# One core, linear attention and a gated SSM: conversion of the second weight unit moved ahead, two tensors turned in 64x64 quarters, a branch that places PE's program, and another order of PSUM banks

## The chip, the cores and the metric

One core of a Trainium2 chip runs the kernel. The metric is device microseconds of one execution, median of several. TensorE is PE here (its weight loads PEld), VectorE is DVE, ScalarE ACT, GpSimd POOL; SyncE (SP) issues most of the DMAs.

## The reference

```python
q, k, v, alpha: (4, 8, 768, 48)                 # batch, heads, steps, width
for t in range(768):
    state = alpha[:, :, t, :, None] * state + einsum('bhd,bhe->bhde', k[:, :, t], v[:, :, t])
    y[:, :, t] = einsum('bhd,bhde->bhe', q[:, :, t], state)
x = y.transpose(0, 2, 1, 3).reshape(4, 768, 384)
val, gate = split(x @ w_in)                     # w_in (384, 1024)
h = exp(A_log)[0] * h + val[:, t]               # along the steps
out = (silu(gate) * hs) @ w_out                 # w_out (512, 384)
```

The weights come as 64-bit floats and are converted on the chip.

## The kernel before, in words

The 768 steps of each batch are cut into three chunks of 256, so there are N = 12 chunks, m or n = 0 to 11. All matmuls are in fp32. For a chunk, the raw q, k and alpha come in with (head, block of steps) on the partitions and are turned so that the width stands there: by `turned` on PE against an identity for chunks 0 to 2 and the alphas of 3 (`alphas`, `straighten` and `turn_over` call it), by DVE's 32x32 transposes (`turn`, L613) later. `turned` has two ways: PE's transpose (L720 and L721), or two matmuls of 64 columns each per step (L725). ScalarE copies the result out (`copy_turned`, L732). Then, on DVE: `scan_P` (L648) makes the running product of the alphas, `scan_V` (L667) the running inverse, `scaled_k` (Zk, L632) and `scaled_q` (Zq, L623) the scaled tensors. `junk` is a check on ScalarE.

On PE: `scores(m)` multiplies Zk with Zq (L816) into two pairs of banks (s0, s1 and two of the common banks); `masks(m)` (L826 in chunks 0 to 2, L832 later) brings them to SBUF, on DVE under a mask and on ScalarE as they are; `values` (L849), `states` (L881) and `carried` (L862) sum the output of the attention in the banks y0 and y1 (for chunk 0 `first_values`, `first_states`, `first_carried` and `first_join`, which copies to xT); `third` is carried, values, carried and the copies and DMAs (L980) that lay the result out as xT. `project(n, cc)` (L1005), cc = 0 to 3, multiplies xT with one weight unit: a bank for the values, read by a scan on DVE (hh, L1014), and one for the gate, read by ScalarE (sg, L1025). `output(n)` and `output_parts(n)` (L1090) multiply with w_out; the second needs fewer matmuls and adds parts on DVE (L1117 to L1119), the last of them when the next chunk has begun (`next(outs)`).

A weight unit is converted by `low` (ScalarE, L556), `high` (DVE, L562 and L564) and `add_low` (POOL, L569); `load_w` (SP, L456) brings its bits. The load of unit 1 waits for a small memset on DVE (L1196).

No scheduler is at work: each engine runs its instructions in the order in which the code writes them, and `go(count)` takes the next steps of DVE's list of products. PSUM has eight banks: mm0 to mm3, y0, y1 (a and b below) and s0, s1 (s and t). Each call of `bank()` without a tag takes the next letter of a string written by hand, `taken`; who takes a bank waits until its last reader is done. `addr_align(256, x, max_nops=0)` puts PE's next instruction at place x of a block of 256, by a branch over the gap; before, it stands only at L1009, in seven projects (cc = 2).

Of the kernel before, what the change touches and what calls it, by code (L numbers as in the profile page):

```python
# [343 lines left out]
FLOOR = 1e-31  # L344
BLOCK_PLACE = 218


@with_exitstack
def fast(
# [221 lines left out]
    def convert(i):  # L571
        if i not in lows:
            low(i)
        high(i)
        add_low(i)
# [98 lines left out]
    def products(m):  # L674
# [19 lines left out]

    taken = iter("0321032103231023" "1023102310231023" "102310231023" "10"
# [16 lines left out]

    turned_by_transpose = ((0, "k"), (1, "a"), (1, "k"), (1, "q"), (3, "a"))

# [66 lines left out]

    def turn_over(m, name, to):
        for js in halves:
            copy_turned(to, js, turned(m, name, js, bank()))
# [9 lines left out]
    def keep_warm(n, w):  # L794
        t = bank("y0")
        for _ in range(n):
            nc.tensor.matmul(t[:, 0:w], nc.const_aps.tensor(0.0, [C, C], FP32),
                             nc.const_aps.tensor(0.0, [C, w], FP32), start=True, stop=True,
                             skip_group_check=True)
# [20 lines left out]
    def masks(m, cs=range(G)):  # L820
        sc = [[t[:, 0:4 * (L + D)].rearrange("p (h x) -> p h x", h=4) for t in pair] for pair in scs[m]]
        mb = mask[:, None, :]
        if m < NG:
            for c in cs:
                for i in range(2):
                    nc.vector.tensor_mul(As[i][:, c], sc[c][i][:, :, D:], mb.to_broadcast([C, 4, L]))  # L826
                for i in range(2):
                    nc.scalar.activation((K0, dS[m % 2][1])[i][:, c, :, 0:D], sc[c][i][:, :, 0:D], AF.Copy)
            return
# [341 lines left out]

    keep_warm(3, 256)
    first_alphas()
    for t in sums:
# [10 lines left out]
    for c in range(G):  # L1185
        scaled_k(0, tk, V, c)
        scaled_q(0, tq, P, c)
    tk, tq = plain("k"), plain("q")
# [6 lines left out]
    high(0)  # L1195
    nc.vector.memset(wbits[units[1]][0:1, 0, 0, 0:1, 0], 0)  # L1196
    load_w(units[1], nc.sync)
    add_low(0)
    copy_turned(tk, halves[1], part)
    first_values(True)  # L1200
    st = states(0)
    part = turned(1, "q", halves[0], bank())
    first_states(st)
    copy_turned(tq, halves[0], part)
    nc.scalar.activation(raws["a"][0:1, 0:1], sums[3][0:1, 0, 0:1], AF.Copy)
    load_steps("a", 2, [nc.sync])
# [8 lines left out]
    first_carried((2, 3))  # L1215
    part = turned(1, "q", halves[1], bank(), False)
    first_join()
    low(1)
    copy_turned(tq, halves[1], part)
    nc.scalar.activation(a_dec, a_log, AF.Exp)  # L1220
    nc.scalar.activation(spare, minus, AF.Silu)
    load_v(2, nc.sync)
    junk(0)

# [12 lines left out]
    for n in range(N):  # L1237
        m = n + 1
        if n == 0:
            V = scan_V(1, P)  # L1240
            high(1)
            fs_late = [project(n, 0)]
            add_low(1)
            alphas(2)
            scaled_k(1, tk, V)
            scaled_q(1, tq, P)
            low(2)
            fs_late.append(project(n, 1))
            convert(2)
            first(m)  # L1250
            tk = straighten(2, "k")
            P = scan_P(2)
            tq = straighten(2, "q")
# [62 lines left out]
        else:  # L1316
            ahead = n > 2
            if n == 2:
                go(1)
            else:  # L1320
                if m + 1 < N:
                    go(1)
                    load_raw("k", n + 3, nc.sync)
                go(2 if ahead else 1)
                next(outs, None)
            if n == N - 2:
# [138 lines left out]
```

## Time and profile before

| | |
|---|---|
| median of 3 runs | 272.77 us (272.77, 273.12, 270.95) |
| profiled execution | 272.92 us, span 270.9 us |
| busy: PE, PEld, DVE, ACT, POOL | 97%, 86%, 88%, 42%, 57% of the span |
| chain that ended last | PE 71%, DVE 17%, DMA 4%, issue 4% |
| moved by DMA | 41.23 MB, mean 152 GB/s |

How to read the lines: in a timeline a row has its start and length in us, engine, line, operation, out<-in and count; in brackets is the idle time of the engine before it and what ended it. A row of waits has the total, the count and the longest. PE records two instructions for each fp32 matmul, so 6 matmuls are x12. The row PEclk has the granted clock of PE in tenths, 9 being full.

### The profile page before, as it was taken

How to read it: one execution, taken by the hardware profiler on the slowest of the kernel's cores; microseconds unless marked ns; L12 is line 12 of the kernel's file. 1: busy time of each engine (PE TensorE's matmuls, PEld its weight loads, DVE VectorE, ACT ScalarE, POOL GpSimd, SP SyncE). 2: the span in 40 equal slices, each digit the busy share in tenths (PEclk: the TensorE clock that was granted, in tenths of full speed). 3: DMA queues.
4: the chain of work that ended last, by engine and by line, in shares of the span. 5: the costliest groups of instructions: out<-in, count | busy, mean ns of one | idle time of the engine just before them, and what ended most of it. 6: DMA issues, size and time to landing. Idle time of an engine off the chain costs nothing.

```text
span 270.9 us, 10035 instructions
## 1 busy us (share of the span) xinstructions
PE 263.5 (97%) x4172; PEld 232.9 (86%) x4172; DVE 239.1 (88%) x326; ACT 112.4 (42%) x272; POOL 154.4 (57%) x195
## 2 busy tenths in 40 slices
PE   8999999999999799999999999999999999999994
PEld 6988888876688688998988988988978989989884
DVE  7979998998999978999999999999999996793452
ACT  3667766462342341731631812713533714414121
POOL 8122323175259745795975895995594995736110
PEclk9999999999999799999999999999999999999999
DMA  6938984998980694189299298498595550211201
GB/s 174 322 123 260 293 174 154 229 204 175 255 202 4 161 222 109 31 211 224 74 230 219 60 235 200 91 224 183 124 229 140 114 162 2 61 43 29 76 6 59
DMA packets 52307, 41.23 MB, mean 152 GB/s; under 512 B 27392, under 2 KB 50944, under 8 KB 52256
## 3 DMA queue, kind: packets, MB, share of 16 engines
q1 hardware_dynamic: 49472, 37.53, 56.7%
q0 software_dynamic: 1536, 2.20, 3.1%
q10 hardware_dynamic: 1248, 0.79, 1.2%
q8 instruction: 36, 0.59, 0.9%
q14 instruction: 15, 0.12, 0.1%
HBM read 32.54 MB, written 4.72 MB: 138 GB/s over the span
## 4 chain that ended last, share of the span: by engine, by line
PE 71%; DVE 17%; DMA 4%; issue 4%; ACT 1%; SPq 1%; POOL 1%; DVEq 0%; POOLq 0%; ACTq 0%
PE mm L1005 25%; PE mm L1090 10%; PE s L1005 7%; PE y L1005 5%; DVE P L648 4%; DMA raw_q<-in_q_dram 4%; PE mm L1041 4%; PE y L1090 3%; PE s L816 3%; PE mm L816 2%; DVE k L613 2%; DVE al L613 2%; PE s L881 2%; PE y L849 2%; PE y L862 2%
## 5 line engine op out<-in xcount | busy, mean ns | idle before, releaser
L1005 PE MATMUL mm<-xT,w_in 128*128 128x256 f32 x384 | 88.9, 383 | 0.7 <-DVE o_sb L1118 0.6
L1005 PEld LDWEIGHTS mm<-xT,w_in 128*128 128x128 f32 x384 | 71.8, 190 | 11.8 <-DVE o_sb L1118 1.0
L1027 POOL TENSOR_TENSOR f_last<-sg,hh 128x256 f32<-128x256 f32 x36 | 28.9, 808 | 30.9 <-DVE hh L1014 18.7
L1025 ACT ACTIVATE sg<-mm 128x256 f32<-128x256 f32 x29 | 11.1, 384 | 56.2 <-PE mm L1005 53.9
L903 POOL TENSOR_TENSOR sum<-sum,dS 128x192 f32<-128x192 f32 x30 | 27.3, 909 | 5.7 <-ACT dS L890 3.8
L667 DVE TENSOR_TENSOR_SCAN V<-al,ends 128x1028 f32<-128x1028 f32 x12 | 28.3, 2358 | 0.4
L648 DVE TENSOR_TENSOR_SCAN P<-al,lower 128x1028 f32<-128x1028 f32 x12 | 28.3, 2355 | 0.3
L1005 PE MATMUL s<-xT,w_in 128*128 128x256 f32 x120 | 28.0, 379 | 0.0
L1005 PEld LDWEIGHTS s<-xT,w_in 128*128 128x128 f32 x120 | 22.7, 190 | 2.8
L980 POOL DMA_DIRECT2D xT<-yst x44 | 22.6, 519 | 3.5 <-ACT yst L977 3.2
L569 POOL TENSOR_TENSOR w_in<-w_in,wr 128x768 int32<-128x768 int32 x4 | 7.3, 1824 | 25.7 <-DVE wr L564 16.1
L1090 PE MATMUL mm<-w_out,f_last 128*128 128x192 f32 x80 | 17.9, 348 | 1.9 <-DVE wobits L832 1.8
L613 DVE STREAM_TRANSPOSE q<-raw_q 128x1024 f32<-128x1024 f32 x9 | 18.3, 2036 | 0.9 <-DMA raw_q<-in_q_dram 0.9
L613 DVE STREAM_TRANSPOSE k<-raw_k 128x1024 f32<-128x1024 f32 x9 | 18.4, 2043 | 0.0
L632 DVE TENSOR_TENSOR Zk<-k,V 128x1024 f32<-128x1024 f32 (+1 forms) x14 | 18.0, 1286 | 0.1
L1025 ACT ACTIVATE sg<-s 128x256 f32<-128x256 f32 x13 | 5.0, 384 | 31.3 <-PE s L1005 28.1
L1014 DVE TENSOR_TENSOR_SCAN hh<-a_dec,hh,mm 128x256 f32<-128x256 f32 x21 | 15.5, 736 | 1.6 <-PE mm L1005 1.6
L1005 PE MATMUL y<-xT,w_in 128*128 128x256 f32 x72 | 16.5, 379 | 0.0
L613 DVE STREAM_TRANSPOSE al<-raw_a 128x1024 f32<-128x1024 f32 x8 | 16.4, 2050 | 0.0
L623 DVE TENSOR_TENSOR Zq<-q,P 128x1024 f32<-128x1024 f32 (+1 forms) x14 | 16.0, 1142 | 0.3
L1090 PEld LDWEIGHTS mm<-w_out,f_last 128*128 128x128 f32 x80 | 13.7, 197 | 2.8 <-DVE wobits L832 2.0
L1005 PEld LDWEIGHTS y<-xT,w_in 128*128 128x128 f32 x72 | 13.7, 190 | 1.9
(232 smaller groups left out, 587.1 us busy)
## 6 DMA issues: line engine op xcount, KB each, us to landing
out_dram<-o_sb SPq DMA_DIRECT2D x23, 192.0 KB, 3.7
v<-in_v_dram SPq DMA_DIRECT2D x22, 192.0 KB, 4.2
raw_k<-in_k_dram SPq DMA_DIRECT2D x18, 184.0 KB, 6.1
raw_q<-in_q_dram SPq DMA_DIRECT2D x18, 184.0 KB, 4.9
raw_k<-in_k_dram SPq DMA_DIRECT2D x18, 176.0 KB, 6.4
raw_q<-in_q_dram SPq DMA_DIRECT2D x18, 176.0 KB, 5.0
wbits<-in_moe_w_in_dram SPq DMA_DIRECT2D x8, 384.0 KB, 5.1
raw_a<-in_alpha_dram SPq DMA_DIRECT2D x16, 184.0 KB, 5.5
```

The lines of the kernel that those rows point to most:

```text
L613: nc.vector.transpose(out=by_runs(to).rearrange("p h c j -> p h j c"), in_=raws[name][:, 0:4 * ROW].rearrange("p (h j d) -> p h j d", h=4, ...
L623: nc.vector.tensor_mul(Zqs[m % 2][:, ds(u0, n), :, D:].rearrange("p u h t -> p h u t"), t[:, :, at].rearrange("p h (u t) -> p h u t", t=L) ...
L632: nc.vector.tensor_mul(Zks[m][:, ds(c0, n)].rearrange("p c h t -> p h c t"), t[:, :, at].rearrange("p h (c t) -> p h c t", t=C), V[:, :, 1 ...
L648: nc.vector.tensor_tensor_scan(out=P, data0=al[:, 0:4 * GP], data1=lower.rearrange("p h t -> p (h t)"), initial=0.0, op0=ALU.mult, op1=ALU ...
L667: nc.vector.tensor_tensor_scan(out=V[:, ::-1], data0=al[:, 1:4 * GP + 1][:, ::-1], data1=ends.rearrange("p h t -> p (h t)")[:, ::-1], init ...
L903: nc.gpsimd.tensor_add(Ss[j][:, :, 0:D], Ss[j - 1][:, :, 0:D], part)
L980: engines[n % len(engines)].dma_start(out=xT[to, a], in_=st[rows, i, e])
L1005: nc.tensor.matmul((pv, pg)[vg], w_ins[cc][:, kk, vg, :], xT[:, kk, :], start=(kk == 0), stop=(kk == NK - 1))
L1014: nc.vector.tensor_tensor_scan(out=hh, data0=a_dec[:, cc:cc + 1].to_broadcast([C, GC]), data1=pv, initial=prev_h[cc][:, GC - 1:GC] if n % ...
L1025: nc.scalar.activation(sg, pg, AF.Silu)
L1027: f = lambda: engine.tensor_mul(fs[n][cc], sg, hh)
L1090: nc.tensor.matmul(o, a[:, k], b[k] if type(b) is list else b[:, k], start=start and k == 0, stop=k == KC - 1, skip_group_check=True)
```

## The change

- In the opening, the memset and the load of weight unit 1 move from behind `add_low(0)` to behind the first Zk; `high(1)`, `low(1)` and `add_low(1)` move ahead of `scan_P(1)`. Both halves of q of chunk 1 are turned together, and by transposes; `junk(0)` goes ahead of `first_join`. One `low(2)` less is written, since `convert(2)` has it, and `convert(2)` goes ahead of project(0, 1), `scan_P(2)` ahead of the scores of chunk 1.
- Alpha and k of chunk 2 are turned in quarters: 32 matmuls on 64x64 tiles in two banks, each bank copied out whole. q of chunk 2 is turned by transposes, in banks y0 and y1.
- `masks` has another order of its copies and multiplications in chunks 0 to 2.
- `taken` has another order of banks at the output of chunk 2 and the projects of chunks 3, 5 and 8.
- In chunk 3 the last output additions of chunk 2 go ahead of `scan_V(5)`.
- PE branches to place 31 of a block behind `keep_warm`.

```diff
+OPENING_PLACE = 31
...
-    taken = iter("0321032103231023" "1023102310231023" "102310231023" "10"
-                 "23012301" "23" "2301" "ab" "2s3t0123" "23" "01" "23ba"
-                 "st23ab23" "23" "23ab" "01" "2s3tab23" "23" "ab" "2310"
+    taken = iter("0321032103231023" "102310ab10231023" "102310231023" "10"
+                 "23012301" "23" "0132" "ab" "0st12301" "23" "01" "23ba"
+                 "st23ab23" "23" "23ab" "01" "2st3ab23" "23" "ab" "2310"
                  "st230123" "23" "01" "23ba" "st23ab23" "23" "23ab" "01"
-                 "2s3tab23" "23" "ab" "2310" "st230123" "23" "01" "23ba"
+                 "2st3ab23" "23" "ab" "2310" "st230123" "23" "01" "23ba"
...
-    turned_by_transpose = ((0, "k"), (1, "a"), (1, "k"), (1, "q"), (3, "a"))
+    turned_by_transpose = ((0, "k"), (1, "a"), (1, "k"), (1, "q"), (2, "q"), (3, "a"))
+    turned_by_quarters = ((2, "a"), (2, "k"))
...
     def turn_over(m, name, to):
+        if (m, name) in turned_by_quarters:
+            raw = steps_of(name, m)
+            parts = [t.rearrange("p (j x) -> p j x", x=64) for t in bank_pair()]
+            for j in range(NJ):
+                for i, r in ((0, 0), (1, 1), (1, 0), (0, 1)):
+                    rows = ds(64 * r, 64)
+                    nc.tensor.matmul(parts[r][ds(64 * i, 64), j], raw[rows, ds(i * ROW + j * D, 64)],
+                                     ident[rows, rows], start=True, stop=True, skip_group_check=True)
+            for r, part in enumerate(parts):
+                nc.scalar.activation(by_runs(to)[:, :, ds(16 * r, 16)],
+                                     part.rearrange("p j (c h) -> p h c j", h=4), AF.Copy)
+            return
...
                 for i in range(2):
+                    if m == 1:
+                        nc.scalar.activation((K0, dS[m % 2][1])[i][:, c, :, 0:D], sc[c][i][:, :, 0:D], AF.Copy)
                     nc.vector.tensor_mul(As[i][:, c], sc[c][i][:, :, D:], mb.to_broadcast([C, 4, L]))
-                for i in range(2):
-                    nc.scalar.activation((K0, dS[m % 2][1])[i][:, c, :, 0:D], sc[c][i][:, :, 0:D], AF.Copy)
+                    if m != 1:
+                        nc.scalar.activation((K0, dS[m % 2][1])[1 - i][:, c, :, 0:D], sc[c][1 - i][:, :, 0:D], AF.Copy)
...
     keep_warm(3, 256)
+    nc.tensor.addr_align(256, OPENING_PLACE, max_nops=0)
     first_alphas()
...
         scaled_k(0, tk, V, c)
+        if not c:
+            nc.vector.memset(wbits[units[1]][0:1, 0, 0, 0:1, 0], 0)
+            load_w(units[1], nc.sync)
         scaled_q(0, tq, P, c)
...
-    nc.vector.memset(wbits[units[1]][0:1, 0, 0, 0:1, 0], 0)
-    load_w(units[1], nc.sync)
     add_low(0)
...
-    part = turned(1, "q", halves[0], bank())
+    parts = [turned(1, "q", js, bank()) for js in halves]
+    high(1)
     first_states(st)
-    copy_turned(tq, halves[0], part)
-    nc.scalar.activation(raws["a"][0:1, 0:1], sums[3][0:1, 0, 0:1], AF.Copy)
+    low(1)
+    add_low(1)
+    for js, part in zip(halves, parts):
+        copy_turned(tq, js, part)
+        if js.start == 0:
+            nc.scalar.activation(raws["a"][0:1, 0:1], sums[3][0:1, 0, 0:1], AF.Copy)
...
-    part = turned(1, "q", halves[1], bank(), False)
+    junk(0)
     first_join()
-    low(1)
-    copy_turned(tq, halves[1], part)
...
-    junk(0)
...
             V = scan_V(1, P)
-            high(1)
             fs_late = [project(n, 0)]
-            add_low(1)
             alphas(2)
             scaled_k(1, tk, V)
             scaled_q(1, tq, P)
-            low(2)
+            convert(2)
             fs_late.append(project(n, 1))
-            convert(2)
+            P = scan_P(2)
             first(m)
             tk = straighten(2, "k")
-            P = scan_P(2)
...
-                go(2 if ahead else 1)
-                next(outs, None)
+                go(1)
+                if n == 3:
+                    next(outs)
+                go(1)
+                if n > 3:
+                    next(outs, None)
```

DVE's order in the opening, from the masks of chunk 0 to Zq of chunk 1 (Zq_118), before. w_in_96 and w_in_97 are units 0 and 1, wide_S and sum the states of chunk 0:

```order
L826 TENSOR_TENSOR AK<-mm,mask 128x4x64
L562 TENSOR_SCALAR w_in_96<-wbits_100 128x768
L564 TENSOR_SCALAR wr<-wbits_100 128x768
L1196 MEMSET wbits_101 1x1
L952 TENSOR_TENSOR wide_S_72<-s_327,wide_S_71 128x4x48
...
L667 SCALAR_TENSOR_TENSOR V<-al_130,ends 128x1028
L658 COPY lower<-P 128x4
L562 TENSOR_SCALAR w_in_97<-wbits_101 128x768
L564 TENSOR_SCALAR wr<-wbits_101 128x768
L1014 SCALAR_TENSOR_TENSOR hh<-a_dec,mm 128x256
L632 TENSOR_TENSOR Zk<-k,V 128x4x2x128
L623 TENSOR_TENSOR Zq_118<-q,P 128x4x4x64
```

The same stretch of DVE with the change:

```order
L842 TENSOR_TENSOR AK<-mm,mask 128x4x64
L563 TENSOR_SCALAR w_in_96<-wbits_100 128x768
L565 TENSOR_SCALAR wr<-wbits_100 128x768
L563 TENSOR_SCALAR w_in_97<-wbits_101 128x768
L565 TENSOR_SCALAR wr<-wbits_101 128x768
L968 TENSOR_TENSOR wide_S_72<-s_331,wide_S_71 128x4x48
...
L668 SCALAR_TENSOR_TENSOR V<-al_130,ends 128x1028
L659 COPY lower<-P 128x4
L1030 SCALAR_TENSOR_TENSOR hh<-a_dec,mm 128x256
L633 TENSOR_TENSOR Zk<-k,V 128x4x2x128
L624 TENSOR_TENSOR Zq_118<-q,P 128x4x4x64
```

The two conversions of unit 1 have moved ahead of the states of chunk 0, and the memset (L1205 there) further up, behind the first Zk.

PE's order from the end of chunk 0's carried (y) to the scores of chunk 1, before:

```order
L943 MATMUL y_388<-Zq_117,wide_S_73 64x64
L725 MATMUL mm<-ident,raw_q 64x128 x8
L1005 MATMUL mm<-xT,w_in_96 128x256 x6
L725 MATMUL mm<-ident,raw_a 64x128 x16
L1005 MATMUL mm<-xT,w_in_97 128x256 x6
L816 MATMUL s_620<-Zq_118,Zk 64x112
```

and with the change:

```order
L959 MATMUL y_390<-Zq_117,wide_S_73 64x64
L1021 MATMUL mm<-xT,w_in_96 128x256 x6
L791 MATMUL mm<-ident,raw_a 64x64 x32
L1021 MATMUL mm<-xT,w_in_97 128x256 x6
L830 MATMUL s_639<-Zq_118,Zk 64x112
```

The second half of q (8 matmuls) no longer stands between chunk 0 and its projection, and the 16 matmuls of alpha of chunk 2 have become 32 small ones.

## The prediction

> **What bounds the kernel now.** I read the page first: busy shares and the granted clock by slice.
>
> ```profile
> PE 263.5 (97%) x4172; PEld 232.9 (86%) x4172; DVE 239.1 (88%) x326; ACT 112.4 (42%) x272; POOL 154.4 (57%) x195
> PEclk9999999999999799999999999999999999999999
> ```
>
> TensorE (PE) is the bound, so only two things shorten the kernel: less PE work in a stage where PE waits for nobody, or a PE wait taken away. One slice, the fourteenth, has a clock below full. So next the waits of PE, longest first, and PE's timeline at the long ones.
>
> ```profile
> PE mm L1090 <- DVE wobits L832: 1.8, 1, 1.8
> ...
> 87.36 0.95 PE L816 MATMUL mm<-Zq,Zk 48*64 48x112 f32 x32
> 90.13 0.92 PE L1090 MATMUL mm<-w_out,f_last 128*128 128x192 f32 x4 [1.82 <-DVE wobits L832]
> ...
> 199.04 1.56 PE L1005 MATMUL mm<-xT,w_in 128*128 128x256 f32 x6 [0.61 <-DVE o_sb L1118]
> ```
>
> In 270.9 us PE waits long in two places: at 88.31, between the scores of chunk 4 and the output of chunk 2, and 0.61 us at the projection of chunk 8. The first has a tail. The windows (columns: length, then busy time and count of PE, PEld, DVE, ACT and POOL, then granted clock, DMA share, GB/s) show it:
>
> ```profile
> 88.00:90.00 2.00, 0.30 (x15) 0.09 (x4) 1.97 (x6) 1.22 (x4) 1.96 (x4) 1.00 0.18 48
> 90.00:92.00 2.00, 1.87 (x9) 1.88 (x10) 2.00 (x3) 0.33 (x1) 1.98 (x4) 0.77 0.51 125
> 92.00:94.00 2.00, 2.00 (x8) 2.00 (x7) 2.00 (x2) 0.66 (x2) 0.26 (x2) 0.50 1.16 271
> 94.00:96.00 2.00, 2.00 (x13) 2.00 (x12) 1.90 (x4) 0.97 (x3) 0.74 (x1) 0.87 1.09 229
> ```
>
> Right behind the idle time the clock is 0.77, 0.50 and 0.87 in three windows of 2 us: 2 x (0.23 + 0.50 + 0.13) = 1.72 us of PE time lost. The 0.61 us wait at 199.04 has no such tail on the clock row. Together the first wait costs 1.82 + 1.72 = 3.54 us.
>
> **The banks (term A).** The wait is for PSUM. The output of chunk 2 takes banks 2 and 3 first, and those hold the second pair of score blocks of chunk 4, which VectorE (DVE) reads last, at the end of this row:
>
> ```profile
> 85.54 0.38 ACT L1025 ACTIVATE sg<-mm 128x256 f32<-128x256 f32 x1 [2.27 <-PE mm L1005]
> ...
> 85.93 0.73 DVE L1014 TENSOR_TENSOR_SCAN hh<-a_dec,hh,mm 128x256 f32<-128x256 f32 x1
> ...
> 89.66 0.41 DVE L832 TENSOR_TENSOR wobits<-mm,mask 128x256 f32<-128x256 f32 x1
> ```
>
> 89.66 + 0.41 = 90.07; PE goes on at 90.13. After the change this output starts in banks 0 and 1, last read by the gate and the scan of project(2, 3), at 85.92 and 86.66, both before PE has finished the scores at 88.31. So the wait ends, and nothing else holds PE there. On PE alone that is 3.54 us.
>
> Can DVE follow? It is the next engine, and PE would run into it. DVE's own waits in the next blocks are its room:
>
> ```profile
> 99.50 0.69 DVE L1014 TENSOR_TENSOR_SCAN hh<-a_dec,mm 128x256 f32<-128x256 f32 x1 [1.29 <-PE mm L1005]
> ...
> 102.09 0.69 DVE L1014 TENSOR_TENSOR_SCAN hh<-a_dec,mm 128x256 f32<-128x256 f32 x1 [0.49 <-PE mm L1005]
> ...
> 110.69 0.42 DVE L832 TENSOR_TENSOR A<-mm,mask 128x256 f32<-128x256 f32 x1 [0.34 <-ACT K L831]
> ...
> 130.10 0.42 DVE L832 TENSOR_TENSOR wobits<-mm,mask 128x256 f32<-128x256 f32 x1 [0.16 <-ACT K L831]
> ...
> 130.96 0.92 PE L1090 MATMUL mm<-w_out,f_last 128*128 128x192 f32 x4
> ```
>
> These waits are for work that PE releases, and an earlier PE takes them away: 1.29 + 0.49 + 0.34 + 0.16 = 2.28 us by the masks of chunk 6. There the output of chunk 4 still starts in banks 2 and 3: PE may start once the DVE row ends (130.52) and did so at 130.96, 0.44 later. So by chunk 4 PE can keep 2.28 + 0.44 = 2.7 us of the 3.54. That is the value I take; the ends are 1.82 (the idle time alone) and 3.54. The three output additions on DVE that now stand before scan_V(5) cost nothing: DVE does them anyway, and PE needs their banks only at project(3, 1) and later.
>
> **Chunk 8 (term B).** Project(8, 1) first writes bank 3, which the o_sb addition frees; now it starts in t and takes bank 3 for its second half, three matmuls later, which is 1.56 us by that row. The 0.61 us go: I take 0.6, with 0 as the other end, if DVE is late by more than that. In projects 3 and 5 the same swap removes nothing, since PE does not wait there.
>
> **The opening (term C).** Here PE gets less work, but DVE decides. The turning by pairs of 64-column matmuls, and two rows for 64x64 tiles, in the chain of waits:
>
> ```profile
> 32.09 3.64 PE mm L725 x64
> ...
> 42.20 0.47 PE y L849 x32
> ```
>
> Two tensors in 3.64 us, 1.82 each. Quarters are 64 records of 64 columns on 64x64 tiles, as L849: 2 x 0.47 = 0.94 each (bounds 0.9 to 1.82, if the four tiles did not overlap). Two tensors: 1.76 less. The two q halves by transposes change about 0.1. This gain counts only if DVE delivers the scaled tensors of chunk 2 sooner, and on DVE work is moved:
>
> ```profile
> 18.23 0.36 DVE L952 TENSOR_TENSOR wide_S<-s,wide_S 128x192 f32<-128x192 f32 x1 [1.06 <-ACT wide_S L950]
> ...
> 19.43 2.29 DVE L648 TENSOR_TENSOR_SCAN P<-al,lower 128x1028 f32<-128x1028 f32 x1
> ...
> 24.44 0.55 DVE L562 TENSOR_SCALAR w_in<-wbits 128x768 uint32<-128x768 uint32 x1
> ...
> 25.41 0.67 DVE L1014 TENSOR_TENSOR_SCAN hh<-a_dec,mm 128x256 f32<-128x256 f32 x1
> 26.00 2.57 DVE L632 TENSOR_TENSOR Zk<-k,V 128x1024 f32<-128x1024 f32 x1
> ...
> 32.81 2.59 DVE L648 TENSOR_TENSOR_SCAN P<-al,lower 128x1028 f32<-128x1028 f32 x1
> ...
> 42.92 0.68 DVE L623 TENSOR_TENSOR Zq<-q,P 128x512 f32<-128x512 f32 x1
> ...
> 61.24 1.21 DVE L632 TENSOR_TENSOR Zk<-k,V 128x1024 f32<-128x1024 f32 x1
> ...
> 17.66 1.82 POOL L569 TENSOR_TENSOR w_in<-w_in,wr 128x768 int32<-128x768 int32 x1 [9.58 <-ACT wr L556]
> 25.65 1.83 POOL L569 TENSOR_TENSOR w_in<-w_in,wr 128x768 int32<-128x768 int32 x1 [6.17 <-DVE wr L564]
> 31.42 1.83 POOL L569 TENSOR_TENSOR w_in<-w_in,wr 128x768 int32<-128x768 int32 x1 [3.94 <-DVE wr L564]
> ...
> 43.95 0.95 PE L816 MATMUL mm<-Zq,Zk 48*64 48x112 f32 x32
> ```
>
> High(1) takes 25.41 - 24.44 = 0.97 and moves into the idle 1.06 us before 18.23: 0.97 gained. Zk takes 2.57 beside POOL's addition at 25.65 (overlap 1.48 us) and 1.21 alone: 1.36 gained, as that addition moves. But it moves behind the first one, to about 19.5 to 21.3, under P(1), which starts at 19.43. What overlap costs a scan shows at 32.81: 2.59 against 2.29 with 0.44 us of overlap, 0.68 per us; Zk paid 1.36 / 1.48 = 0.92. For 1.8 us: 1.2 to 1.7 lost. P(2) now runs ahead of the masks, right behind high(2), so POOL's third addition overlaps it by about 1.3 us in place of 0.44: 0.6 to 0.8 lost. Net for DVE: 0.97 + 1.36 - 1.45 - 0.7 = 0.2 us. PE's second scores of chunk 2 start at 43.95, 0.35 behind Zq's end (43.60), and can come up by that much more: 0.5 us for the opening. It can go lower, by the moved load:
>
> ```profile
> SPq L456 <- DVE wbits L1196: 7.7, 1, 7.7
> ...
> DMA to landing us min/median/max: 3.3/5.1/6.8
> ```
>
> The queue of SP waits for the memset; behind the first Zk that stands at about 12.4, so the second half is issued near 13.0 and lands at 16.3 to 19.8 by the spread of these eight transfers, median 18.1. High(1) wants it at 17.2. Up to 18.1 the delay vanishes, since P(1) waits for POOL anyway; at 19.8 DVE is 1.5 to 1.7 late: an opening of -1.2. The other end is PE's 1.7 us with no contention. Low(1) and junk on ScalarE now stand ahead of the copies of xT, which PE awaits, but in idle time that is there:
>
> ```profile
> 21.73 0.39 ACT L957 ACTIVATE xT<-y 128x256 f32<-128x256 f32 x1 [1.79 <-PE y L943]
> ```
>
> The new order of the masks lets ScalarE and DVE read different banks at once; PE's next matmuls need DVE's four rows as before, so I cost it at nothing.
>
> **The branch.** It costs what the seven at L1009 cost:
>
> ```profile
> L1009 PEldq COMPARE_BRANCH  x7: 183/183/214, 99.3 to 218.7; - x7
> ...
> 1.00 2.92 PE L797 MATMUL y<-const-float32-0.0 128*128 128x256 f32 x6 [1.00 <-PEq L1449]
> 4.04 1.22 PE L741 MATMUL s<-ident,raw_a 64*64 64x64 f32 x26
> ```
>
> 0.2 us on PE's sequencer, while the array does the three warming matmuls until 3.92. Nothing, unless its target has first to be fetched (below).
>
> **Sum.** The profiled execution took 272.92 us, 2.0 more than its span, and 0.15 more than the median of 272.77. 2.7 + 0.6 + 0.5 = 3.8: 272.92 - 3.8 = 269.1.
>
> **Rivals.** (1) DVE keeps up wholly, as its contention with POOL happens to fall better: 0.8 + 3.54 + 0.6 = 4.9, 268.0. For it: the 0.44 us at the output of chunk 4 is the only place so tight that I found. Against: DVE is busy 48.0 of 50 us in the blocks that follow:
>
> ```profile
> 100.00:150.00 50.00, 50.00 (x800) 45.08 (x802) 48.00 (x53) 18.47 (x49) 35.66 (x44) 1.00 0.68 156
> ```
>
>  (2) The clock does not fall because of the wait, and falls anyway: 0.5 + 1.82 + 0.6 = 2.9, 270.0. For it: the drop starts only after PE is at work again. Against: it is the one drop on the row, and it follows the one long idle time. [...] (3) The load of unit 1 lands near 19.8: -1.2 + 2.7 + 0.6 = 2.1, 270.8. (4) The wait comes back in the next block: PE arrives 3.5 us early at the scores of chunk 5, DVE gets there only 1.3 us sooner because q or Zq is held up by POOL, and over 1.8 us of idle time brings the slow clock again: 0.5 + 1.3 - 0.3 = 1.5, 271.4. (5) Slower: the branch misses. [...] The 183 to 214 ns, with no gap behind any of the seven, speak against it, though there PE has some 4 us of queued work.
>
> [...]
>
> **How the numbers follow.** Forecast 0.45, (1) 0.2, (2) 0.13, (3) 0.09, (4) 0.08, (5) 0.05. About 1% (2.7 us, below 270.0) is what a measurement of this kernel tells from no change, as the runs shown span 2.2 us. Faster: the forecast, (1), and part of (2): 0.70. Slower: (5) and a little: 0.06. The rest, 0.24, is the same. The range goes from 267.5, DVE free and an opening of 1.3, to 271.2, which takes in (2) and (3) and about half of (4).
>
> **What would show it.** Right: no idle time before the first L1090 behind the scores of chunk 4, and a full clock row there; the first L741 near 4.04; POOL's second L569 near 19 to 21.5, Zk of chunk 1 near 1.2 us, P(1) and P(2) over 2.9; PE waiting a few tenths for DVE in blocks 3 and 4, most at the output of chunk 4; no wait at project(8, 1). Wrong: a PE wait over 1 us in block 3, a dip of the clock row, high(1) waiting for its load past 18.5, or L741 late.

## The result, and the profile after

The change gives 271.24 us (median of 20 runs) against 273.37 us before (20 runs): ratio 0.9936, interval 0.9909 to 0.9963, so 0.6% faster. The ratios and intervals, here and below, leave out the slow runs (over 1.5% above the fastest of the same kernel; of the change one, of 939.05 us), the medians count every run. The forecast was 269.1 us in a range of 267.5 to 271.2; the result lies just above the range, and inside the 1% that the forecast put as the border of what can be told from no change. By the medians 2.1 us are gained, where 3.7 were forecast. The profiled execution of the change took 269.95 us (span 268.2), less than its median, and 3.0 us under the profiled one of before.

The page's busy shares and clock, and then the longest waits of PE (total, count, longest):

```profile
PE 260.9 (97%) x4212; PEld 231.3 (86%) x4212; DVE 240.8 (90%) x326; ACT 112.5 (42%) x272; POOL 159.1 (59%) x195
PEclk9999999999999999999999999999999999999999
```

```profile
PE mm L1021 <- ACT xT L973: 1.0, 1, 1.0
PE y L811 <- PEq L1470: 1.0, 1, 1.0
PE s L743 <- DMA raw_a<-in_alpha_dram: 0.7, 1, 0.7
PE s L830 <- DVE Zq L624: 0.4, 1, 0.4
PE mm L1021 <- DVE hh L1030: 0.3, 1, 0.3
```

The two waits that the change aims at, 1.82 and 0.61 us, are gone, and so is the dip of the clock. What is new stands in the opening: PE waits 0.7 us for the first alphas and 1.0 us for xT. The place of the first wait, in the timeline and in the windows:

```profile
88.93 0.95 PE L830 MATMUL mm<-Zq,Zk 48*64 48x112 f32 x32
89.81 0.92 PE L1106 MATMUL mm<-w_out,f_last 128*128 128x192 f32 x4
...
90.00:92.00 2.00, 2.00 (x13) 2.00 (x13) 1.97 (x6) 1.42 (x5) 1.96 (x5) 1.00 0.27 74
92.00:94.00 2.00, 2.00 (x15) 2.00 (x14) 2.00 (x2) 1.30 (x4) 1.98 (x4) 1.00 0.76 163
94.00:96.00 2.00, 2.00 (x101) 1.72 (x100) 2.00 (x2) 0.00 (x1) 2.00 (x1) 1.00 1.15 275
```

The output of chunk 2 follows the scores of chunk 4 without idle time, at full clock. The opening, PE first, then DVE and POOL:

```profile
4.60 1.22 PE L743 MATMUL s<-ident,raw_a 64*64 64x64 f32 x26 [0.68 <-DMA raw_a<-in_alpha_dram]
...
6.92 2.65 PE L770 MATMUL mm<-ident,raw_q 128*64 128x128 f32 x24
```

```profile
18.91 1.59 DVE L563 TENSOR_SCALAR w_in<-wbits 128x768 uint32<-128x768 uint32 x1 [0.85 <-DMA wbits<-in_moe_w_in_dram]
...
22.09 3.05 DVE L649 TENSOR_TENSOR_SCAN P<-al,lower 128x1028 f32<-128x1028 f32 x1
...
28.45 1.20 DVE L633 TENSOR_TENSOR Zk<-k,V 128x1024 f32<-128x1024 f32 x1
...
32.26 3.65 DVE L649 TENSOR_TENSOR_SCAN P<-al,lower 128x1028 f32<-128x1028 f32 x1
...
44.59 0.68 DVE L624 TENSOR_TENSOR Zq<-q,P 128x512 f32<-128x512 f32 x1
...
18.24 1.84 POOL L570 TENSOR_TENSOR w_in<-w_in,wr 128x768 int32<-128x768 int32 x1 [10.17 <-DVE wr L565]
21.16 1.82 POOL L570 TENSOR_TENSOR w_in<-w_in,wr 128x768 int32<-128x768 int32 x1 [1.08 <-DVE wr L565]
31.92 1.83 POOL L570 TENSOR_TENSOR w_in<-w_in,wr 128x768 int32<-128x768 int32 x1 [8.94 <-DVE wr L565]
```

Each of the three long DVE rows (high(1), P(1) and P(2)) lies in part under a POOL addition, and the load of unit 1 lands late: high(1) starts at 18.91. The first work on alphas starts at 4.60 in place of 4.04. Starts of the same work of PE show where the time went:

| start of | before | after | difference |
|---|---|---|---|
| first scores | 13.18 | 14.42 | +1.24 |
| scores of chunk 4 | 86.59 | 88.16 | +1.57 |
| scores of chunk 5 | 108.45 | 106.45 | -2.00 |
| scores of chunk 9 | 186.32 | 184.39 | -1.93 |
| scores of chunk 10 | 207.01 | 204.31 | -2.70 |

From chunk 4 to 5 the banks bring 3.57 us, from 9 to 10 another 0.77. The opening costs 1.57 us, where 0.5 us of gain was forecast. DVE sets that time: its last Zq of chunk 2 ends at 45.27 in place of 43.61, and PE waits 0.4 us for it, in the list above.

### The profile page after: what moved, and what is told of

Read it like the earlier page. It is cut to its first block, busy times and chain, and to the rows that moved or that the text cites. A ratio compares the mean times of both kernels' runs of the same rounds, so it can differ in the third digit from the quotient of the medians.

```text
span 268.2 us, 10116 instructions
## 1 busy us (share of the span) xinstructions
PE 260.9 (97%) x4212; PEld 231.3 (86%) x4212; DVE 240.8 (90%) x326; ACT 112.5 (42%) x272; POOL 159.1 (59%) x195
## 3 DMA queue, kind: packets, MB, share of 16 engines
HBM read 32.54 MB, written 4.72 MB: 139 GB/s over the span
## 4 chain that ended last, share of the span: by engine, by line
PE 79%; DVE 12%; DMA 5%; issue 3%; SPq 0%; ACT 0%; DVEq 0%; ACTq 0%
PE mm L1021 27%; PE mm L1106 13%; PE s L1021 9%; PE y L1021 5%; PE y L1106 4%; PE mm L1057 4%; PE s L830 3%; PE s L897 3%; PE mm L830 3%; DVE P L649 2%; PE y L865 2%; DMA wbits<-in_moe_w_in_dram 2%; PE y L878 2%; PE mm L865 2%; DVE hh L1030 2%
## 5 line engine op out<-in xcount | busy, mean ns | idle before, releaser
L1041 ACT ACTIVATE sg<-mm 128x256 f32<-128x256 f32 x32 | 12.3, 384 | 63.5 <-PE mm L1021 61.3
L649 DVE TENSOR_TENSOR_SCAN P<-al,lower 128x1028 f32<-128x1028 f32 x12 | 30.5, 2542 | 0.2
L919 POOL TENSOR_TENSOR sum<-sum,dS 128x192 f32<-128x192 f32 x30 | 28.3, 944 | 2.1 <-ACT dS L906 0.3
L1106 PE MATMUL mm<-w_out,f_last 128*128 128x192 f32 x80 | 17.3, 338 | 0.3
L633 DVE TENSOR_TENSOR Zk<-k,V 128x1024 f32<-128x1024 f32 (+1 forms) x14 | 16.8, 1199 | 0.1
L1131 POOL TENSOR_TENSOR wide_S<-wide_S,wr 128x192 f32<-128x192 f32 x9 | 13.9, 1548 | 3.3 <-ACT wr L1114 3.2
L624 DVE TENSOR_TENSOR Zq<-q,P 128x1024 f32<-128x1024 f32 (+1 forms) x14 | 15.5, 1104 | 0.3
L1030 DVE TENSOR_TENSOR_SCAN hh<-a_dec,hh,mm 128x256 f32<-128x256 f32 x19 | 14.0, 735 | 1.8 <-PE mm L1021 1.8
L1106 PEld LDWEIGHTS mm<-w_out,f_last 128*128 128x128 f32 x80 | 13.0, 189 | 1.2 <-issue 0.5
```

The source lines that it names most:

```text
L624: nc.vector.tensor_mul(Zqs[m % 2][:, ds(u0, n), :, D:].rearrange("p u h t -> p h u t"), t[:, :, at].rearrange("p h (u t) -> p h u t", t=L) ...
L633: nc.vector.tensor_mul(Zks[m][:, ds(c0, n)].rearrange("p c h t -> p h c t"), t[:, :, at].rearrange("p h (c t) -> p h c t", t=C), V[:, :, 1 ...
L649: nc.vector.tensor_tensor_scan(out=P, data0=al[:, 0:4 * GP], data1=lower.rearrange("p h t -> p (h t)"), initial=0.0, op0=ALU.mult, op1=ALU ...
L919: nc.gpsimd.tensor_add(Ss[j][:, :, 0:D], Ss[j - 1][:, :, 0:D], part)
L1030: nc.vector.tensor_tensor_scan(out=hh, data0=a_dec[:, cc:cc + 1].to_broadcast([C, GC]), data1=pv, initial=prev_h[cc][:, GC - 1:GC] if n % ...
L1106: nc.tensor.matmul(o, a[:, k], b[k] if type(b) is list else b[:, k], start=start and k == 0, stop=k == KC - 1, skip_group_check=True)
```

## The experiments

The theory: both bank edits do all they can, and the opening gives part of it back, by the branch and by work that DVE now does beside POOL's additions. The numbers of all kernels follow, the times within the kernel from one profile each. "Stretch" goes from the end of DVE's first Zq to the end of the last Zq of chunk 2, and so leaves the start of the opening out; "4 to 5" is the time between the starts of these scores; "0 to 3" that from the output of chunk 0 (its matmuls on f_last) to the scores of chunk 3. Each ratio is to runs of before on the same chip (medians 273.79 us for e1 to e4, 273.20 for e5 to e8, 274.21 for e9 to e12), so it is not the quotient of two medians of the table.

| kernel | first alphas landed | first scores | stretch | 0 to 3 | 4 to 5 | span | median us | ratio to before |
|---|---|---|---|---|---|---|---|---|
| before | 3.91 | 13.18 | 30.58 | 5.25 | 21.87 | 270.9 | 273.37 | 1 |
| the change | 4.46 | 14.42 | 31.43 | 5.25 | 18.29 | 268.2 | 271.24 | 0.9936 |
| e1_banks | 4.16 | 13.19 | 30.57 | 6.71 | 18.34 | 268.5 | 269.86 | 0.9891 (0.9840 to 0.9943) |
| e2_branch | 5.06 | 15.53 | 30.59 | 6.95 | 22.29 | 274.8 | 275.58 | 1.0017 (0.9969 to 1.0064) |
| e3_nobranch | 3.73 | 12.95 | 31.42 | 5.25 | 18.29 | 267.4 | 270.41 | 0.9902 (0.9867 to 0.9936) |
| e4_unit1 | 4.72 | 14.56 | 31.13 | 5.25 | 18.29 | 269.9 | 270.45 | 0.9910 (0.9879 to 0.9941) |
| e5_old_p2 | 3.76 | 13.46 | 31.32 | 5.55 | 18.34 | 269.2 | 270.81 | 0.9895 (0.9815 to 0.9975) |
| e6_no_quarters | 4.06 | 13.20 | 31.42 | 5.25 | 18.29 | 267.2 | 269.59 | 0.9887 (0.9826 to 0.9948) |
| e7_banks_quarters | 3.94 | 13.39 | 31.00 | 5.25 | 18.29 | 267.4 | 269.88 | 0.9896 (0.9848 to 0.9944) |
| e8_branch_later | 3.87 | 13.31 | 31.39 | 5.25 | 18.29 | 268.2 | 272.76 | 0.9943 (0.9894 to 0.9992) |
| e9_no_add | 4.01 | 12.96 | 29.83 | 5.25 | 18.39 | 267.9 | | |
| e10_before_no_add | 4.02 | 13.20 | 30.51 | 5.25 | 21.86 | 272.6 | | |
| e11_banks_junk | 3.92 | 13.54 | 30.57 | 5.25 | 18.29 | 266.9 | 269.29 | 0.9855 (0.9803 to 0.9907) |
| e12_after_again | 4.83 | 14.91 | 31.43 | 5.25 | 18.29 | 269.7 | 271.33 | 0.9909 (0.9874 to 0.9943) |

**The banks alone.** The kernel before with these edits:

```diff
-                 "23012301" "23" "2301" "ab" "2s3t0123" "23" "01" "23ba"
+                 "23012301" "23" "0132" "ab" "0st12301" "23" "01" "23ba"
...
-                 ... "2s3tab23" ...          # in two lines
+                 ... "2st3ab23" ...
```

and the output additions in chunk 3 ahead of scan_V(5).

> The kernel before with only the new order of banks at the later outputs and projects, and the three output additions of chunk 2 ahead of scan_V(5); opening untouched, no branch in the opening. Theory: this part of the change works fully (PE idle 1.82 us and the slow clock behind it gone, 3.5 us; project(8, 1) some 0.7 us) and the opening of the changed kernel gave 1.6 us back. Then this kernel is faster than the changed one: profiled span about 270.9 - 4.3 = 266.6, time about 268.5, ratio to before 0.982 to 0.987; no idle time between the scores of chunk 4 and the output of chunk 2. Rival: the bank part is worth only what the changed kernel shows in all (about 2 to 3 us) and the opening is neutral: about 270.3, ratio 0.990 or above.

PE goes on at once behind the scores of chunk 4, and 4 to 5 takes 18.34: the 3.5 us are the banks'. The span is 1.9 us above what was expected, 1.5 of it because of something neither theory had: 0 to 3 took 6.71 in place of 5.25. DVE, POOL and PE of this kernel there:

```profile
52.91 0.56 DVE L562 TENSOR_SCALAR w_out<-wobits 128x768 uint32<-128x768 uint32 x1
53.38 2.28 DVE L564 TENSOR_SCALAR wr<-wobits 128x768 uint16<-128x768 uint16 x1
...
53.29 1.88 POOL L569 TENSOR_TENSOR w_out<-w_out,wr 128x768 int32<-128x768 int32 x1 [6.93 <-ACT wr L556]
...
71.55 1.56 PE L1041 MATMUL mm<-w_out,f_last 128*128 128x384 f32 x4 [1.19 <-DVE f_last L1027]
```

and the same work of the kernel before:

```profile
53.33 0.61 DVE L564 TENSOR_SCALAR wr<-wobits 128x768 uint16<-128x768 uint16 x1
...
53.28 4.32 POOL L569 TENSOR_TENSOR w_out<-w_out,wr 128x768 int32<-128x768 int32 x2 [6.91 <-ACT wr L556]
```

POOL's addition begins within 0.1 us of DVE's row. In e1_banks DVE loses and takes 2.28 us, to 0.5 us behind the end of POOL's row; before, DVE has its 0.61 us and POOL's two additions take 4.32 in place of 2 x 1.83. e5_old_p2 falls as e1_banks does; in the nine other traces with the new banks DVE keeps its 0.6 us. So each can take longer beside the other, DVE's row by 1.67 us and POOL's two additions by 0.66. Which of them does, the traces show; why, they do not. Here are DVE and POOL of e5_old_p2 and then of e6_no_quarters:

```profile
54.09 2.26 DVE L565 TENSOR_SCALAR wr<-wobits 128x768 uint16<-128x768 uint16 x1
...
53.90 1.97 POOL L570 TENSOR_TENSOR w_out<-w_out,wr 128x768 int32<-128x768 int32 x1 [7.34 <-ACT wr L557]
```

```profile
54.24 0.61 DVE L565 TENSOR_SCALAR wr<-wobits 128x768 uint16<-128x768 uint16 x1
...
54.05 4.43 POOL L570 TENSOR_TENSOR w_out<-w_out,wr 128x768 int32<-128x768 int32 x2 [7.35 <-DVE wr L565]
```

POOL's record begins 0.19 us before DVE's in both, and DVE loses in the first and wins in the second. So the winner can't be read from the starts, and can differ between traces in which these rows begin alike.

e2_branch, with the old banks, shows the same contention one row earlier: there the second load of wobits lands late, DVE's L563 begins at 55.31, 0.09 us behind POOL's row, and takes 2.18 us. PE then waits 1.43 us, and 0 to 3 is 6.95.

**The branch.**

```diff
 # e2_branch: the kernel before, with
+    nc.tensor.addr_align(256, OPENING_PLACE, max_nops=0)   # behind keep_warm
 # e3_nobranch: the changed kernel, with
-    nc.tensor.addr_align(256, OPENING_PLACE, max_nops=0)
 # e8_branch_later: the changed kernel, with that line behind first_alphas()
 # e12_after_again: the changed kernel
```

> The kernel before with only the branch behind keep_warm. Theory: the branch leads to a block of instructions that must be fetched at once: 16 KB on the instruction queue near 2.0 us, beside the first alphas, which land at about 4.46 in place of 3.91; PE idles 0.6 us, the clock gate opens later (57 ns per record only from about 8.4 us in place of 5.8), the first scores start at about 14.4 in place of 13.18, and the time is 0.8 to 1.6 us more: ratio 1.003 to 1.006. Rival: the late alphas and the late clock of the changed kernel's profile were chance of that one execution: first alphas at 3.9, first scores at 13.2, ratio 1.000 within 0.002.

> The changed kernel without the branch. Theory: no fetch near 2.0 us, first alphas at about 3.9, first scores at about 13.2, and all behind it 0.8 to 1.2 us sooner: profiled span about 267.2, ratio to before 0.987 to 0.990 (the changed kernel: 0.9936). Rival: the same as the changed kernel, ratio 0.993 to 0.994. A third: the branch also spares fetches in mid-opening, so that without it PE shows gaps with no releaser elsewhere and the time is longer.

> The changed kernel with the branch moved behind the first alphas' matmuls. Theory: it is the fetch of 16 KB beside the first alphas that costs, not the branch: first alphas land near 3.9 as without a branch, the fetch starts at 4 us or later, first scores within 0.3 us of e3_nobranch's 12.95 unless the fetch now delays the raw q (then up to 13.6), ratio 0.989 to 0.991. Rival: the branch itself stalls TensorE until its block is there: an idle gap of about 1 to 2 us behind the first alphas, first scores later than 14, ratio 0.993 or more.

> The changed kernel once more, beside the others on one chip. Theory: again a fetch of 16 KB between 2.0 and 2.7 us, first alphas 1.4 to 1.6 us behind the end of that fetch, first scores between 14.3 and 15.6; ratio 0.991 to 0.996, so slower than e11_banks_junk by 0.7% or more. Rival: this time the alphas land before 4.0 beside the same fetch, which would make the late alphas of three profiles chance.

The instruction queue of the changed kernel in the first 4 us (packets, MB, share of 16 engines), and that of e12_after_again:

```profile
q8 instruction: 1, 0.02, 1.5%
```

```profile
q8 instruction: 1, 0.02, 2.1%
```

One packet of 16 KB. The kernels with the branch behind keep_warm all have it there, and no other kernel has one before 8 us. By the packets' times it runs from 2.03 to 2.96 in the changed kernel, 2.67 to 3.61 in e2_branch, 2.04 to 3.17 in e4_unit1 and 2.08 to 3.39 in e12_after_again, and the first alphas land at 4.46, 5.06, 4.72 and 4.83: 1.4 to 1.6 us behind the end of the fetch each time. In the ten others they land at 3.73 to 4.16. PE goes on about 0.14 us behind the landing of the alphas each time; then its 24 records on raw_q take 2.65 us in place of 2.14 (2.53 to 3.18 in the four, 1.96 to 2.43 in the ten), and the first scores start at 14.4 to 15.5 in place of 12.9 to 13.5. By the clock events of the traces PE has its full clock from 8.37 to 10.03 us on in the four, and from 3.82 to 7.18 in the ten. So the late alphas were no chance.

That it is the fetch which delays them, and not the branch as such, is argued from this order of times: their transfer is issued at 0.90 us on ScalarE's queue in every kernel, ahead of PE's branch (1.03). e8_branch_later fits, with alphas at 3.87 and first scores at 13.31, but does not separate the two: behind its branch (5.38) no block of 16 KB comes before 8.60, where e11_banks_junk has one (8.61) without a branch there.

Still the time of e8_branch_later is no better, 272.76 us, and its runs spread from 269.64 to 275.06. Its profiled execution took 270.15 us and has waits of PE with no releaser, of up to 0.8 us. The mean granted clock is on record for each run: seven of the twelve have 0.999 or 1.000, with a median of 270.42 us, and five have 0.985 to 0.994, with 274.24. So a fall of the clock goes with the longer runs. No trace shows which wait brings it, and the rest of what they lose stays open.

In time e2_branch can't be told from before (interval on both sides of 1), though the median of all its runs is 1.8 us above that of before on the same chip. Its profile is of a run of 276.73 us, and 1.7 us of its span are the contention named above. Without the branch the change measured 270.41 against 271.24 and 271.33 with it; as ratios 0.9902 against 0.9936 and 0.9909, with overlapping intervals. So the size rests on the traces, where the scores of chunk 4 start at 87.19 without it and at 88.16 and 89.25 with it.

**The moved steps of the opening.** e4_unit1 is without the move of unit 1, e5_old_p2 without that of convert(2) and scan_P(2), e7_banks_quarters without both, and e6_no_quarters without the quarters. e4_unit1 keeps the branch, the other three do not have it.

```diff
 # e4_unit1: memset, load_w, high(1), low(1), add_low(1) where they were before
 # e5_old_p2: no branch, and
-            convert(2)
             fs_late.append(project(n, 1))
-            P = scan_P(2)
+            convert(2)
             first(m)
             tk = straighten(2, "k")
+            P = scan_P(2)
 # e7_banks_quarters: no branch, and both
 # e6_no_quarters: no branch, and
-    turned_by_quarters = ((2, "a"), (2, "k"))
+    turned_by_quarters = ()
```

> The changed kernel with the conversion of weight unit 1 back in its old places (memset and load behind high(0); low(1), high(1) and add_low(1) as before), the branch kept. Theory: the move is what delayed VectorE by 0.9 us more than the late start explains (0.85 us waiting for the load, high(1) 1.59 us beside POOL's first addition, P(1) 3.05 us beside the second): the last Zq of chunk 2 ends about 0.5 to 1.0 us sooner than in the changed kernel (45.27), ratio 0.989 to 0.992. Rival: what is lost in the opening is only the late start and P(2) beside POOL's third addition (3.65 us), and the move is neutral: Zq ends at 45.0 to 45.5, ratio 0.993 to 0.995.

> The changed kernel without the branch, and with convert(2) and scan_P(2) back in their old places (convert(2) behind project(0, 1), scan_P(2) behind the scores and masks of chunk 1). Theory: scan_P(2) ahead of the masks runs beside POOL's third addition (3.65 us in the changed kernel, 2.59 before), which is what VectorE still loses without the branch (from the first to the last Zq of the opening 30.21 us in e3_nobranch, 29.37 in before): P(2) back under 2.7 us, the last Zq of chunk 2 0.5 to 0.8 us sooner relative to the first, time 0.5 us under that of e3_nobranch, ratio 0.987 to 0.989. Rival: POOL's addition only meets something else (the masks or the first scan), nothing changes: ratio 0.990.

> The changed kernel without the branch and with both groups of moved steps of the opening back in place (unit 1 as before; convert(2) and scan_P(2) as before): what stays of the change is the quarters, the transposes of q, the order of the masks and the banks. Theory: VectorE gets its old order and the opening is that of before or 0.2 to 0.5 us sooner (last Zq of chunk 2 at 43.2 to 43.7), all bank gains kept: profiled span 266.2 to 267, ratio 0.982 to 0.988, the fastest of all. Rival: without high(1) in the idle microsecond, Zk of chunk 1 meets POOL again (2.57 us) and it is no faster than e3_nobranch: ratio 0.990.

> The changed kernel without the branch, and with alpha and k of chunk 2 turned by the old pairs of 64-column matmuls in place of 64x64 quarters. Theory: VectorE sets the pace of the opening, so 1.2 to 1.8 us more work on TensorE is hidden but for a few tenths: first to last Zq of the opening within 0.3 us of e3_nobranch, ratio 0.990 to 0.992. Rival: TensorE is as tight there and up to 1.2 us come out at the end: ratio 0.993 to 0.995.

The move of unit 1 costs 0.3 us of stretch (31.43 to 31.13, and 31.32 to 31.00), not the 0.5 to 1.0 expected: it takes Zk of chunk 1 out from beside POOL, as forecast, but puts high(1) and P(1) there. Nor does the last Zq of e4_unit1 end sooner: at 45.23, as its rival had it, since its alphas landed later still.

In e5_old_p2 P(2) is back at 2.53 us and the stretch is only 0.1 us shorter, so that theory falls; behind the masks P(2) starts later by what it saves. Both undone leave 31.00, still 0.4 over before, and e7_banks_quarters is not the fastest kernel, as was expected, but at the 0.990 of its rival. Zk of chunk 1 takes 2.31 and P(2) 2.53 there, beside POOL, no more than before. What is new is a wait of DVE at the first mask of chunk 1:

```profile
32.20 0.42 DVE L842 TENSOR_TENSOR A<-s,mask 128x256 f32<-128x256 f32 x1 [0.71 <-ACT K L841]
```

In e5_old_p2 it is 0.74 us, and before there is none (31.37). The new order of the masks puts ScalarE's copy ahead of DVE's multiplication in chunk 1, so it is the likely cause; no run has that order alone. The quarters bring nothing: without them the stretch is the same 31.42.

**POOL's additions.** `add_low` returns at once for the four units of w_in. One execution each: 269.89 and 274.52 us.

```diff
     def add_low(i):
+        if i < NI:
+            return lows.pop(i)
```

> The changed kernel without the branch and without POOL's four additions to w_in (the low bits of the input weights are left out). Theory: what VectorE still loses in the opening of the change is time beside these additions: high(1) 0.99 in place of 0.55, P(1) 3.05 and P(2) 3.65 in place of 2.30 in e3_nobranch, 2.55 us in all. Without them these rows fall to 0.55 and 2.3, and the stretch from the end of the first Zq to the end of the last Zq of the opening goes from 31.41 to about 28.9. Rival: VectorE waits for the load of unit 1 and for TensorE instead: the stretch falls by less than 1 us, to 30.5 or more.

> The kernel before without POOL's four additions to w_in (the low bits of the input weights are left out). Theory: before, only Zk of chunk 1 (2.57) and P(2) (2.59) lie beside them, 1.65 us: the same stretch goes from 30.58 to about 28.9, so that with no additions the two openings are equal within 0.3 us. Rival: the openings differ for another reason (load, masks), and this one comes out 0.5 us or more shorter or longer than e9_no_add.

DVE in the opening of e9_no_add:

```profile
18.56 0.56 DVE L563 TENSOR_SCALAR w_in<-wbits 128x768 uint32<-128x768 uint32 x1 [1.53 <-DMA wbits<-in_moe_w_in_dram]
...
20.72 2.29 DVE L651 TENSOR_TENSOR_SCAN P<-al,lower 128x1028 f32<-128x1028 f32 x1
...
30.63 2.28 DVE L651 TENSOR_TENSOR_SCAN P<-al,lower 128x1028 f32<-128x1028 f32 x1
```

The three rows are at their free lengths, as expected. Of the 2.55 us, 1.59 come out of the stretch (31.42 to 29.83); the rest goes into waits. The wait for the load of unit 1 before high(1) is not new, 1.53 us in place of 1.43 in e3_nobranch. The kernel before does not shorten at all (30.58 to 30.51): there its rows fall to 1.20 and 2.29 too, and DVE waits for PE instead:

```profile
29.25 0.69 DVE L1016 TENSOR_TENSOR_SCAN hh<-a_dec,mm 128x256 f32<-128x256 f32 x1 [0.81 <-PE mm L1007]
...
31.49 0.42 DVE L828 TENSOR_TENSOR A<-s,mask 128x256 f32<-128x256 f32 x1 [0.58 <-PE s L818]
```

So the expectation of two equal openings was wrong. Free of POOL, DVE's stretch of the change is 0.7 us shorter than that of before; with POOL it is 0.8 us longer. Before, DVE's time beside POOL was hidden behind PE; the change takes work from PE, and DVE's time shows.

That is DVE's time alone. On PE e9_no_add gains next to nothing: the first scores start at 12.96 and those of chunk 4 at 87.07, against 12.95 and 87.19 in e3_nobranch, and against 13.20 and 86.71 in e10_before_no_add.

```profile
PE y L867 <- DMA v<-in_v_dram: 0.9, 1, 0.9
...
87.07 0.95 PE L832 MATMUL s<-Zq,Zk 48*64 48x112 f32 x32
```

In this one execution PE waits 0.92 us for a load of v, at 37.32, and the scores of chunk 2 start 0.85 us behind DVE's last Zq. So the runs show what POOL costs DVE, and not how much of it would come off the time.

**POOL's addition beside DVE's row, and the best version.** e1_banks with one line moved:

```diff
-            convert(4)
             junk(2)
+            convert(4)
             low(5)
```

> e1_banks with junk(2) on ScalarE ahead of convert(4), so that the low bits of the first unit of w_out, and with them POOL's addition, come 1.1 us later, behind VectorE's conversion of the second. Theory: in e1_banks POOL's addition began at 53.29, 0.09 us before VectorE's L564, which then took 2.28 in place of 0.61 us and made TensorE wait 1.19 us at 71.55; before, the same two rows fell the other way round. With the new order L564 takes 0.6 each time, from the output of chunk 0 to the scores of chunk 3 it is 5.2 us in place of 6.7, profiled span about 267.0, ratio 0.980 to 0.987. Rival: the addition then holds up the three f_last products or the transposes instead, and span and time are those of e1_banks (268.5, 0.989).

```profile
53.84 0.60 DVE L564 TENSOR_SCALAR wr<-wobits 128x768 uint16<-128x768 uint16 x1
54.33 0.73 DVE L1014 TENSOR_TENSOR_SCAN hh<-a_dec,hh,mm 128x256 f32<-128x256 f32 x1
54.98 1.80 DVE L1027 TENSOR_TENSOR f_last<-sg,hh 128x256 f32<-128x256 f32 x1
...
54.66 3.81 POOL L569 TENSOR_TENSOR w_out<-w_out,wr 128x768 int32<-128x768 int32 x2 [8.05 <-ACT wr L556]
```

POOL starts at 54.66, behind DVE's row of 0.60; the f_last products pay 0.4 us (1.80, before 1.42), no more. 0 to 3 is 5.25 again, the span 266.9, the time 269.29 us (268.99 to 269.65 in six runs), ratio 0.9855 (0.9803 to 0.9907). That is the lowest median of all, with the banks and this line and nothing of the new opening, though its interval overlaps with those of e1_banks, e6_no_quarters and e7_banks_quarters; the changed kernel on the same chip took 271.33.

## Why the prediction was wrong

**Term A, the banks:** mechanism right, size too small. Forecast 2.7, measured 3.57 (4 to 5: 21.87 to 18.29). The limit by DVE did not hold at its tight place, the output of chunk 4:

```profile
128.60 0.43 DVE L848 TENSOR_TENSOR wobits<-mm,mask 128x256 f32<-128x256 f32 x1
...
129.17 0.89 PE L1106 MATMUL mm<-w_out,f_last 128*128 128x192 f32 x4
```

PE still starts behind DVE's masks (129.03), but counted from the scores of chunk 4 DVE is there 3.06 us sooner than before (40.87 against 43.93), where the forecast gave it its 2.28 us of waits and no more; where the other 0.8 us came from was not followed up. PE loses 0.2 us there and has them back by the next scores. Rival (1) was right on this term in the number; whether for its reason, POOL's contention, is not shown.

Rival (2), a fall of the clock without the wait, is not borne out: none of the eleven profiles of the new order of banks has a fall behind these scores, while the three of the old order have one, behind waits of 1.82, 2.20 and 1.82 us. The windows of e2_branch:

```profile
92.00:94.00 2.00, 0.42 (x19) 0.20 (x10) 1.97 (x4) 1.28 (x4) 1.88 (x4) 1.00 0.12 31
94.00:96.00 2.00, 1.38 (x6) 1.39 (x7) 2.00 (x3) 0.33 (x1) 1.98 (x5) 0.84 0.38 100
96.00:98.00 2.00, 2.00 (x8) 2.00 (x8) 2.00 (x2) 0.33 (x1) 0.67 (x1) 0.50 0.99 210
98.00:100.00 2.00, 2.00 (x12) 2.00 (x11) 1.90 (x4) 1.12 (x4) 0.60 (x1) 0.81 1.09 247
```

By the clock events of the three traces the half clock lasts 3.41 us each time (91.10 to 94.51 before), and each stretch of full clock in the fourteen traces is a whole multiple of it (25 times, 85.33 us, ahead of the fall). So in these traces the clock changes at the borders of windows of 3.41 us. The window ahead of the half clock holds the whole wait; PE was busy in it for 1.59, 1.21 and 1.59 us. Half of 3.41 us is 1.71; the forecast had read 1.72. So PE was at work for more than a third of each of these windows, and the half clock came all the same. Waits of 1.19 us (e1_banks) and 1.43 us (e2_branch) had no fall behind them. From what wait on the clock falls, the traces do not show.

The fall is likely behind the wait, not certain. Of the 75 runs with the old order of banks whose clock is on record 47 have a mean of 0.994 or less, about what one such window takes off (1.71 of 271 us); of the 94 with the new order it is 6, and none of them has a trace. In before alone it is 38 of 62, with a median of 274.20 us, against 272.55 in the other 24. So a forecast from one profile with a fall takes too much: by that share the fall costs 1.0 us on average, not 1.7 (an estimate from these runs).

**Term B, chunk 8:** right, 0.77 for 0.6, with no wait at project(8, 1) left.

**Term C, the opening:** this is the step that failed, -1.57 (and -2.66 in the second profile of the same kernel, where the scores of chunk 4 start at 89.25) for +0.5, outside its bounds of -1.2 to +1.7. It has two parts, 0.8 us up to the end of DVE's first Zq (13.84 in place of 13.03) and 0.85 us from there on:

- *The branch* was costed at "nothing, unless its target has first to be fetched"; that the branch misses, rival (5), had a chance of 0.05. A block was fetched in all four profiles, in 0.9 to 1.3 us. None of the four shows PE standing for it: in the changed kernel the warming matmuls run from 1.00 to 3.92 as before, and behind them PE waits 0.68 us for the first alphas. These land late beside the fetch, by 0.5 to 1.1 us in the four, with 0.5 us of slower PE records behind (changed kernel). The cover by the warming matmuls was reckoned for PE alone; what else moves by DMA at 2 us was not asked.
- *DVE's sum*: a gain of 0.2 forecast, 0.8 lost (stretch 30.58 to 31.43). Zk came out as said (1.20). High(1) was not to meet POOL's first addition: the load (landed at 18.89, between the median and the late end that the text had) put it there, 0.85 us late and 1.59 long, so the idle 1.06 us counted as room were not enough. P(1) lost 0.76 us (3.05 for 2.29), less than the 1.2 to 1.7 reckoned; P(2) lost 1.06 more than before (3.65 for 2.59), where 0.6 to 0.8 were reckoned. The prices per us of overlap were about right (0.85 and 0.91 for the 0.89 and 1.49 us that these two overlap POOL); which rows would meet POOL, and for how long, was not.

Low(1) and junk ahead of the copies of xT were put at nothing too: PE waits 1.0 us for xT there (24.43). DVE's hh row behind it follows DVE's own scan without a wait (27.86), so nothing shows that this wait reached the end.

**Why the time missed the range:** 3.57 + 0.77 - 1.57 = 2.77 us, and the profiled span fell by 2.7. That is inside the range, helped by the 0.87 us that term A brought beyond the forecast. With the +0.5 of the forecast the opening would have brought 2.1 us more. The rest is spread: the profile of the change is of a run of 269.95 us, a second one of a run of 271.73 starts the scores of chunk 4 another 1.09 us later, with a longer fetch and a 0.5 us wait of PE without releaser, and the medians lie between the two, at 271.24 and 271.33. The range had no term for that.

Of the named signs, those of the banks, of POOL's second addition (21.16), of Zk and of both scans came out; the waits of a few tenths for DVE in blocks 3 and 4 did not, as the list of PE's waits has none there. L743 at 4.60 was the sign of the branch, and high(1) past 18.5 that of the load.

## What to carry to other kernels

An idle microsecond of one engine is only worth what it is after its inputs and its neighbour have been asked: here it lay in front of a late load and beside a POOL addition. A branch that places code can bring a fetch by DMA at that place (16 KB in 0.9 to 1.3 us here), so ask which load is awaited there, and look at more than one execution; here the kernel without it had a lower median than the one with it moved (270.41 against 272.76). Where a POOL addition and a DVE row began within 0.2 us of one another, 1.7 us fell either way (2.28 us in e1_banks, 0.61 before); move the one that can wait, as e11_banks_junk does. Its six runs lie within 0.7 us, those of e1_banks, on another chip, within 2.6.

## What the runs showed of the hardware

- A fetch of 16 KB of instructions took 0.9 to 1.3 us near the start of the program (the change, e2_branch, e4_unit1, e12_after_again), and a 192 KB load in flight landed 1.4 to 1.6 us behind its end, 0.5 to 1.1 us later than the mean of the ten profiles without it (3.94).
- Three rows of DVE beside a POOL addition of int32 took longer by about the time that they overlapped it: the fp32 scan P(2) 3.65 us for 2.29 with 1.49 us of overlap, the uint32 row of high(1) 1.59 for 0.55 with 1.17 (both in the change), the uint16 row L564 2.28 for 0.61 with 1.79 (e1_banks). With POOL's record 0.05 to 0.19 us ahead of DVE's L564 or L565 DVE lost in two traces (e1_banks, e5_old_p2) and kept its 0.6 us in four (before, e6_no_quarters, e8_branch_later, e9_no_add).
- The granted clock of PE changed in steps of 3.41 us (25 steps at full clock, one at 0.50, 52 at full clock in before), and a window of that length with 1.8 to 2.2 us of waiting in it was followed by one at 0.50 in three of three traces (before, e2_branch, e10_before_no_add); waits of 1.2 us (e1_banks) and 1.4 us (e2_branch) had no such window behind them. Of 62 runs of before 24 had no such fall.
